# Sums and splits moved from GpSimd to VectorE, squares to ScalarE, renamed blocks and new planner costs in a fused retention, expert and feed-forward kernel

## The chip, the cores and the metric

One core of a Trainium2 chip. The metric is device time in microseconds (us) of that core, the median of several executions. "The profiled execution" is one execution recorded by the hardware profiler. The trace uses the engine names PE (TensorE matmuls), PEld (its weight loads), DVE (VectorE), ACT (ScalarE), POOL (GpSimd) and SP (the queue that issues most DMAs).

## What is computed

Three blocks follow each other, on 4,608 tokens (8 sequences of 576, 8 heads of width 64, model width 512):

```python
ret = (scale * q @ k.T) * Dmat                  # decayed, causal retention
x   = (ret @ v), heads joined                   # [4608, 512]
logits = x @ w_gate + modality_bias[modality_id]
e = argmax(logits); g = softmax(logits)[e]
x   = g * (relu(x @ w1[e]) @ w2[e])             # one expert of 8 per token, width 1024
h   = relu(x @ w_in)                            # dense, width 2048
out = (h * h) @ w_out
```

All arithmetic of the reference is float32. The last two blocks are worked out with each float32 operand split into a high part in a rounded format and the rest (hi and lo), three matmuls per product.

## The kernel before

The program runs in three stages on one core.

**Retention stage** (`phase0`, the first 195 us). Token tiles of 128, with routing tables built alongside. The change does not touch it.

**Expert stage** (`phase12`, 195 to 698 us). Tokens are gathered by expert into slots of 512 tokens ("E", 0 to 7) and a last slot of 256 (number 8). A slot has 8 units, and the loop at the end of `phase12` runs over all 80 units `i`. In each unit it emits `first` of the next unit (12 matmuls, then ACT writes `hh` and DVE writes `hl`), `second` of this one (12 matmuls), at four units of a slot the transposes of the next slot's gathered tokens (`trans`, tile `xg`), one expert weight's split (`wsplit`: ACT writes the high part of `wx` or `wy`, DVE the rest) and, through `part(cs, ...)`, a piece of the **conversion**. The gather (`gather`) is four indirect DMAs from POOL's queue, emitted in the first unit of a slot for the next.

The conversion (`convs`) turns the dense weights `w_in` and `w_out`, which arrive as 64-bit floats, into float32 and then into hi and lo blocks. It runs for 16 pieces; of each, `conv1` loads `craw`, `conv2` has six DVE steps on `cwk` (L693 to L707), one ACT square (L698) and four block sums of 256 columns (L715), and `conv3` splits the seven blocks in two parts of 768 and 1024 columns (`split`: ACT writes `cwh` at L149, the given engine `cwl` at L150) and stores them to `wc`. Each `yield` in it is one step (six per piece). Before, `part(cs, 2 if i >= 15 else 0)` runs two steps per unit from unit 15 on, so that the 99 steps take 50 units, and the sums and the splits' lower parts are on POOL.

`combos` makes the seven operand blocks of the dense stage's first token tile from the finished slot E (tile `eyr`), stores them to `xc`, and `preload` reads them back in unit 66.

**Dense stage** (`phase3`, from 698 us). Three passes over 9 token tiles of 512; in a pass, each tile meets three groups (`q`) of the hidden width, in the last pass two. Per group, a seven-product block scheme (Winograd's form of Strassen's) takes two matrix products: `one` has seven products `x`, `two` has seven, each of 6 matmuls of 256 columns. Between them DVE, ACT and POOL turn the seven results of `one` into blocks `z` (relu and square in `sq`, L1099; sums by `tt`, L1096) and split them into `h` (`hsplit`: ACT at L1213, DVE at L1214). `two`'s results are added up in `oe` or `yr`. In pass 0 `xprep` makes the next tile's operand blocks `x` (sums on POOL, splits on ACT and DVE); in the last pass POOL issues the indirect output DMAs (L1250).

The order of the dense stage is written by a list scheduler, `Plan`: every operation has a cost per engine (`a_`, `d_`, `p_`, `m_`) and its dependencies; `emit` picks the operation that can start first by these costs and thereby fixes the order in each engine's queue. An operation with two engines in its list goes to the one where it would end first. Each engine then runs its queue strictly in that order.

```python
            d_ = lambda c: [(DVE_, 0.153 + 0.00104 * c)]
            p_ = lambda c: [(POOL_, 0.10 + 0.00186 * c)]
                    tt(z[:, 3, :], z[:, 1, :], z[:, 0, :], ALU.subtract, 256, kz_(0, 1), kz_(3), p_(256) + d_(256))
```

Of the kernel before, what the change touches and what calls it, by code (L numbers as in the profile page):

```python
# [9 lines left out]
F32 = mybir.dt.float32  # L10
# [5 lines left out]
ALU = mybir.AluOpType  # L16
# [72 lines left out]
def kernel(ctx, tc, qT, kT, kN, vN, modT, w_gate, mbias, w1, w2, w_in, w_out,  # L89
# [574 lines left out]
    def phase12():  # L664
        with ExitStack() as c1:
# [5 lines left out]
            def conv1(i):  # L671
                fp, m = i // 2, i % 2
                raw = CR[i] = cv.tile([P, 2, 2 * CV], I32, tag="w", name="craw")
                for s_ in range(2):
# [4 lines left out]
                    else:  # L679
# [3 lines left out]
                        for j in range(2):  # L683
                            sp.dma_start(dst[:, j], src[s_, :, j])

            def conv2(i):
# [8 lines left out]
                yield 1  # L695
# [3 lines left out]
                yield 1  # L699
                dve.tensor_scalar(out=i1, in0=i2, scalar1=-(1 << 23), scalar2=None, op0=ALU.bitwise_and)  # L700
                yield 1
                dve.scalar_tensor_tensor(out=t1, in0=lw.bitcast(U32), scalar=2.0 ** -52, in1=t1,
                                         op0=ALU.mult, op1=ALU.mult)
                yield 1
                dve.tensor_tensor(out=t2, in0=t2, in1=t1, op=ALU.add)
                yield 1
# [6 lines left out]
                         (7, 3, ALU.subtract, 5)))[i % 2]  # L713
                for o, a, op, b in sums:
                    pool.tensor_tensor(out=bl[o], in0=bl[a], in1=bl[b], op=op)  # L715
                yield 1

            def conv3(i, part):
# [3 lines left out]
                split(ch, cl, src, pool)  # L722
# [21 lines left out]
            def combos():  # L744
                yr = cv.tile([P, KD, TS], F32, tag="w", name="eyr")
                tx = cv.tile([P, 3, 2, 256], F32, tag="w", name="etx")
                sp.dma_start(yr, yd[:, 0:TS].rearrange("(c p) t -> p c t", p=P))
                yield 1
                b11, b12 = yr[:, 0:2, 0:256], yr[:, 0:2, 256:512]
                b21, b22 = yr[:, 2:4, 0:256], yr[:, 2:4, 256:512]  # L750
                for o, a, b in ((tx[:, 0], b12, b11), (tx[:, 1], b22, tx[:, 0]), (b12, b22, b12),
                                (tx[:, 2], b21, tx[:, 1])):
                    pool.tensor_tensor(out=o, in0=a, in1=b, op=ALU.subtract)
                    yield 1
                src = (b11, b21, b22, tx[:, 0], tx[:, 1], b12, tx[:, 2])
                for m in range(7):
                    if m % 2 == 0:
                        xo = cv.tile([P, 2, 2, 2, 256], F32R, tag="w", name="exo")
                    split(xo[:, m % 2, 0], xo[:, m % 2, 1], src[m], dve)
                    sp.dma_start(xc[0, m], xo[:, m % 2].bitcast(F32).rearrange("p a k t -> p (a k t)"))  # L760
                    yield 1

            def preload():
                wload2(0, 0, cv)
                for a in range(4):
                    t_ = cv.tile([P, 2, 2, 2, 256], F32R, tag="w", name=f"x{a}")
                    for m in range(2 * a, min(2 * a + 2, 7)):
# [83 lines left out]
            def convs():  # L851
# [3 lines left out]
                for i in range(NCV + 1):  # L855
# [10 lines left out]
                    for n, _ in enumerate(conv2(i)):  # L866
                        if i and n in (2, 4):
                            conv3(i - 1, n // 4)
# [465 lines left out]
```

## Time and profile before

| | us |
|---|---|
| median of 3 runs (range) | 1500.33 (1497.33 to 1505.33) |
| the profiled execution: its own time | 1501.8 |
| the profiled execution: span of its instructions | 1500.0 |
| PE busy | 1390.7 (93% of the span) |
| DVE busy | 1089.3 (73%) |
| ACT busy | 579.9 (39%) |
| POOL busy | 503.8 (34%) |

A busy time is a union over the span; a busy PE is not a PE at its peak, since matmuls are pipelined. So the text also counts matmuls per stretch. PEclk is the share of TensorE's full clock that was granted: 1.00 is 2.4 GHz, and the lower level of 1.2 GHz counts as 0.50.

### The profile page before, as it was taken

Reading aid. Unit: us, or ns where it says so; the run is one execution under the profiler, and the core shown is the slowest. Engines: PE = TensorE matmul, PEld = TensorE weight load, DVE = VectorE, ACT = ScalarE, POOL = GpSimd, SP = SyncE. Lnnn points to the kernel's source line nnn. Section 1 sums busy time; section 2 is a strip of 40 time slices with the busy share of each in tenths; the row PEclk is TensorE's granted clock in tenths of the full one; section 3 lists DMA queues with packets and bytes.
Section 4 is the critical chain, followed back from the end, with each engine's and each line's share of the span. In section 5 each row is a group of like instructions: output and inputs, shape, how many; then the busy total and the mean of one; then the engine's idle time right before and its main releaser. Section 6 shows DMA issues by size and latency. Waiting matters only on the chain. (4 is left out here: it accounts for less than half of the span.)

```text
span 1500.0 us, 26403 instructions
## 1 busy us (share of the span) xinstructions
PE 1390.7 (93%) x10384; PEld 1263.5 (84%) x10384; DVE 1089.3 (73%) x1744; ACT 579.9 (39%) x1152; POOL 503.8 (34%) x440
## 2 busy tenths in 40 slices
PE   7999999979998989998799999999999999998994
PEld 6889878857776777778799999998999999998994
DVE  3776764649988988843688888867767777686784
ACT  1444443424444444432355444543223332233331
POOL 2222102216555555600434434322112222144354
PEclk9999999989999999999999999999999999999998
DMA  9977247868798889698644455576445564677672
GB/s 343 346 264 277 84 150 195 286 143 214 281 266 247 273 270 274 197 353 199 250 155 155 180 192 215 216 291 227 155 160 194 197 220 157 232 259 275 231 252 87
DMA packets 144743, 336.08 MB, mean 224 GB/s; under 512 B 20321, under 2 KB 54625, under 8 KB 144609
## 3 DMA queue, kind: packets, MB, share of 16 engines
q1 hardware_dynamic: 136528, 313.73, 62.2%
q0 software_dynamic: 5920, 19.40, 3.4%
q8 instruction: 83, 1.36, 0.4%
q10 hardware_dynamic: 2160, 1.17, 0.3%
q14 instruction: 52, 0.42, 0.1%
HBM read 226.24 MB, written 108.02 MB: 223 GB/s over the span
## 5 line engine op out<-in xcount | busy, mean ns | idle before, releaser
L1096 POOL TENSOR_TENSOR z<-z 128x256 f32<-128x256 f32 x176 | 178.9, 1018 | 421.7 <-DVE z L1096 381.7
L1114 PE MATMUL bank<-w,h 128*128 128x256 f32 x1008 | 288.8, 286 | 24.7 <-DVE h L1214 24.7
L1112 PE MATMUL bank<-w,h 128*128 128x256 f32 x1008 | 287.5, 285 | 14.8 <-ACT h L1213 11.9
L1112 PE MATMUL bank<-x,w 128*128 128x256 f32 x1008 | 285.9, 284 | 0.9 <-ACT z L1093 0.9
L1113 PE MATMUL bank<-x,w 128*128 128x256 f32 x1008 | 286.1, 284 | 0.1
L1113 PE MATMUL bank<-w,h 128*128 128x256 f32 x1008 | 284.2, 282 | 1.5 <-DMA w<-wc 1.3
L1114 PE MATMUL bank<-x,w 128*128 128x256 f32 x1008 | 284.9, 283 | 0.0
L1214 DVE TENSOR_TENSOR h<-z,h 128x512 fp32r<-128x512 f32 (+2 forms) x243 | 213.9, 909 | 10.3 <-ACT h L1213 10.1
L1114 PEld LDWEIGHTS bank<-w,h 128*128 128x128 f32 x1008 | 191.1, 190 | 35.1 <-DVE h L1214 35.1
L1213 ACT ACTIVATE h<-z 128x512 fp32r<-128x512 f32 (+2 forms) x243 | 155.5, 646 | 153.3 <-POOL z L1096 102.3
L1112 PEld LDWEIGHTS bank<-w,h 128*128 128x128 f32 x1008 | 191.5, 190 | 19.2 <-ACT h L1213 12.9
L1093 ACT ACTIVATE z<-bank 128x256 f32<-128x256 f32 x288 | 107.6, 380 | 256.9 <-PE bank L1114 256.3
L1113 PEld LDWEIGHTS bank<-x,w 128*128 128x128 f32 x1008 | 192.7, 191 | 1.2 <-DVE x L1096 0.3
L1112 PEld LDWEIGHTS bank<-x,w 128*128 128x128 f32 x1008 | 192.4, 191 | 1.6 <-ACT z L1093 1.4
L1113 PEld LDWEIGHTS bank<-w,h 128*128 128x128 f32 x1008 | 191.2, 190 | 2.1 <-DMA w<-wc 2.1
L1114 PEld LDWEIGHTS bank<-x,w 128*128 128x128 f32 x1008 | 192.8, 191 | 0.0
L775 PE MATMUL bank<-hh,wy 128*128 128x512 f32 (+1 forms) x320 | 131.2, 410 | 15.3 <-ACT hh L791 14.1
L1099 DVE SCALAR_TENSOR_TENSOR z<-z 128x256 f32<-128x256 f32 (+1 forms) x216 | 126.1, 585 | 23.4 <-ACT z L1093 17.2
L776 PE MATMUL bank<-hl,wy 128*128 128x512 f32 (+1 forms) x320 | 128.7, 402 | 6.7 <-DVE hl L792 6.7
L777 PE MATMUL bank<-hh,wy 128*128 128x512 f32 (+1 forms) x320 | 127.4, 398 | 0.0
L775 PE MATMUL bank<-xh,wx 128*128 128x512 f32 (+1 forms) x320 | 124.0, 388 | 2.2 <-PEq L888 1.7
L776 PE MATMUL bank<-xl,wx 128*128 128x512 f32 (+1 forms) x320 | 123.8, 387 | 0.7 <-DVE xl L742 0.7
(167 smaller groups left out, 2414.5 us busy)
## 6 DMA issues: line engine op xcount, KB each, us to landing
x<-xc SPq DMA_DIRECT2D x119, 512.0 KB
wr<-w SPq DMA_DIRECT2D x80, 512.0 KB
w<-wc SPq DMA_DIRECT2D x32, 896.0 KB
xc<-x SPq DMA_DIRECT2D x56, 512.0 KB
wc<-cwh SPq DMA_DIRECT2D x16, 896.0 KB
wc<-cwl SPq DMA_DIRECT2D x16, 896.0 KB
pd<-oe SPq DMA_DIRECT2D x24, 512.0 KB
xd<-xs SPq DMA_DIRECT2D x9, 1024.0 KB
```

Source lines behind the costliest of these rows:

```text
L775: pe.matmul(ps, lh, rh, start=first, stop=False)
L776: pe.matmul(ps, lh, rl, start=False, stop=False)
L777: pe.matmul(ps, ll, rh, start=False, stop=last)
L1093: plan.add(a_(c), lambda e: e.activation(o, i, AF.Copy), r, w)
L1096: plan.add(engs or d_(c), lambda e: e.tensor_tensor(out=o, in0=a, in1=b, op=op), r, w)
L1099: plan.add(d_(c), lambda e: e.scalar_tensor_tensor(out=z, in0=z, scalar=0.0, in1=z, op0=ALU.max, op1=ALU.mult), k, k)
L1112: e.matmul(ps[n], lh, rh, start=first and n == 0, stop=False, skip_group_check=True)
L1113: e.matmul(ps[n], lh, rl, start=False, stop=False, skip_group_check=True)
L1114: e.matmul(ps[n], ll, rh, start=False, stop=True, skip_group_check=True)
L1213: plan.add(a_(c), lambda e: e.activation(h[:, 0, a:b], z[:, a + 1:b + 1], AF.Copy), rs, ks[0])
L1214: plan.add(d_(c), lambda e: e.tensor_tensor(out=h[:, 1, a:b], in0=z[:, a + 1:b + 1], in1=h[:, 0, a:b].bitcast(F32), op=ALU.subtract), rs + ...
```

## The change

- In the conversion, the four block sums and the lower part of the splits go from POOL to DVE. The steps are no longer counted one by one: each `yield` gives a number of columns, and `part(cs, 2250)` hands out 2,250 columns per unit from unit 4 on; the 137,336 columns take 61 units. The two parts of `conv3` come one step earlier within the next piece.
- The copies of a slot's results out of PSUM (`ye`) are all on ACT; before, every other one was on DVE.
- `combos` runs at unit 68 and after, on DVE and ACT, and writes the operand blocks where the dense stage reads them; `preload` with its reading back from `xc` is gone, and the first dense weights are loaded in unit 73 instead of 66.
- In the dense stage the blocks `z` and `h` are renamed (`MH`; the two halves of `w_out` trade places in `conv1`, `dst[:, 1 - j]`), so that the `h` blocks that the first products of `two` read are made from other products of `one`. All sums of `z` are on DVE alone. The product `x == 4` is squared by ACT (relu on the way out of PSUM, then Square in place); the other three squares may go to DVE, or to ACT as two operations.
- The planner's costs change: ACT, DVE and above all POOL (for 256 columns from 0.58 to 0.87 us), and the handover between engines from 0.2 to 0.25 us.

```diff
             def conv2(i):
...
                 for o, a, op, b in sums:
-                    pool.tensor_tensor(out=bl[o], in0=bl[a], in1=bl[b], op=op)
-                yield 1
+                    dve.tensor_tensor(out=bl[o], in0=bl[a], in1=bl[b], op=op)
+                    yield 300
 
             def conv3(i, part):
...
-                split(ch, cl, src, pool)
+                split(ch, cl, src, dve)
...
+                sub(tx, b12, b11)
+                put(0, b11)
+                yield 1
...
                     for c in cols:
-                        if c % 2:
-                            act.activation(ye[:, c, :wd], Y[s, c][:, :wd], AF.Copy)
-                        else:
-                            dve.tensor_copy(ye[:, c, :wd], Y[s, c][:, :wd])
+                        act.activation(ye[:, c, :wd], Y[s, c][:, :wd], AF.Copy)
...
+            spare = [0]
+
             def part(gen, n):
-                while n and next(gen, 0):
-                    n -= 1
+                spare[0] = min(spare[0] + n, 2 * n)
+                while spare[0] > 0:
+                    c_ = next(gen, 0)
+                    if not c_:
+                        return
+                    spare[0] -= c_
                     yield
...
-                    fill(wsg(i + 6, 2 if i < 10 else 1, i + 9), part(cs, 2 if i >= 15 else 0))
-                    if 9 <= i <= 14:
-                        run(ex, 2)
-                    if i == 66:
-                        preload()
+                    fill(wsg(i + 6, 2 if i < 10 else 1, i + 9), part(cs, 2250))
+                    if i >= 68:
+                        run(ex, 3)
+                    if i == 73:
+                        assert next(cs, 0) == 0 and next(ex, 0) == 0
+                        wload2(0, 0, cv)
...
-    MH = {1: 0, 2: 1, 7: 2, 4: 3, 5: 4, 6: 5, 3: 6}
+    MH = {1: 0, 4: 1, 2: 2, 5: 3, 6: 4, 7: 5, 3: 6}
...
-        HAND = 0.2
+        HAND = 0.25
...
-            a_ = lambda c: [(ACT_, 0.17 + 0.00086 * c)]
-            d_ = lambda c: [(DVE_, 0.153 + 0.00104 * c)]
-            p_ = lambda c: [(POOL_, 0.10 + 0.00186 * c)]
+            a_ = lambda c: [(ACT_, 0.21 + 0.00083 * c)]
+            d_ = lambda c: [(DVE_, 0.15 + 0.00106 * c)]
+            p_ = lambda c: [(POOL_, 0.20 + 0.0026 * c)]
...
+                    if e is act:
+                        e.activation(z, z, AF.Relu)
+                        e.activation(z, z, AF.Square)
+                    else:
+                        e.scalar_tensor_tensor(out=z, in0=z, scalar=0.0, in1=z, op0=ALU.max, op1=ALU.mult)
...
-                    copy(z[:, 1, :], X_, 256, [kx], kz_(1))
-                    sq(z[:, 0:2, :], 512, kz_(0, 1))
-                    tt(z[:, 3, :], z[:, 1, :], z[:, 0, :], ALU.subtract, 256, kz_(0, 1), kz_(3), p_(256) + d_(256))
...
+                    copy(z[:, 3, :], X_, 256, [kx], kz_(3), AF.Relu)
+                    copy(z[:, 3, :], z[:, 3, :], 256, kz_(3), kz_(3), AF.Square)
+                    hsplit(u, z, h, 2 if last else 0, 3, kz_)
...
+                    tt(z[:, 4, :], z[:, 0, :], z[:, 2, :], ALU.add, 256, kz_(0, 2), kz_(4))
+                    if last:
+                        hsplit(u, z, h, 3, 4, kz_)
+                    tt(z[:, 5, :], z[:, 4, :], z[:, 1, :], ALU.subtract, 256, kz_(4, 1), kz_(5))
+                    hsplit(u, z, h, 4 if last else 3, 5, kz_)
```

The order that the change makes is shown at three places. The first is POOL's queue in the expert stage, around the gather for one slot (`xg` is the tile of gathered tokens, `ix` its indices, `cwk` and `cwl` the conversion's). Before:

```order
L150 TENSOR_TENSOR cwl<-cwk,cwh 128x768
L150 TENSOR_TENSOR cwl<-cwk,cwh 128x1024
L715 TENSOR_TENSOR cwk<-cwk 128x2x128 x4
L429 TENSOR_LOAD slots
L429 ISA x2
L431 ISA
L431 COPY ix<-tab 128x4
L434 DMA xg<-xd,ix 128x512 x4
L150 TENSOR_TENSOR cwl<-cwk,cwh 128x768
L150 TENSOR_TENSOR cwl<-cwk,cwh 128x1024
```

Now:

```order
L434 DMA xg<-xd,ix 128x512 x4
L429 TENSOR_LOAD slots
L429 ISA x2
L431 ISA
L431 COPY ix<-tab 128x4
L434 DMA xg<-xd,ix 128x512 x4
```

Between two gathers nothing else stands in POOL's queue any more.

The second is DVE's queue in the dense stage, second pass, around the end of `one` and the start of `two` (`z` and `h` are the blocks of three groups in turn, `bank` PSUM). Before:

```order
L1214 TENSOR_TENSOR h_9179<-z_9182,h_9179 128x512
L1214 TENSOR_TENSOR h_9178<-z_9181,h_9178 128x512
L1099 SCALAR_TENSOR_TENSOR z_9183<-z_9183 128x512
L1096 TENSOR_TENSOR z_9183<-z_9183,bank_88 128x256
L1099 SCALAR_TENSOR_TENSOR z_9183<-z_9183 128x256
L1096 TENSOR_TENSOR z_9183<-z_9183 128x256
L1214 TENSOR_TENSOR h_9180<-z_9183,h_9180 128x512
L1214 TENSOR_TENSOR h_9179<-z_9182,h_9179 128x512
L1214 TENSOR_TENSOR h_9180<-z_9183,h_9180 128x512
L1096 TENSOR_TENSOR oe<-oe,bank_85 128x2x256
```

Now:

```order
L1111 TENSOR_TENSOR z_9172<-z_9172,bank_88 128x256
L1236 TENSOR_TENSOR h_9169<-z_9172,h_9169 128x256
L1119 SCALAR_TENSOR_TENSOR z_9172<-z_9172 128x256
L1236 TENSOR_TENSOR h_9168<-z_9171,h_9168 128x512
L1111 TENSOR_TENSOR z_9172<-z_9172 128x256 x2
L1236 TENSOR_TENSOR h_9167<-z_9170,h_9167 128x512
L1236 TENSOR_TENSOR h_9169<-z_9172,h_9169 128x256 x2
L1111 TENSOR_TENSOR oe<-oe,bank_85 128x2x256
L1111 TENSOR_TENSOR z_9171<-z_9171 128x256 x2
L1111 TENSOR_TENSOR z_9172<-z_9172 128x256 x2
```

The sums of the last group (the rows `z<-z` without a bank) now stand in DVE's queue between its splits, and the last group's splits are cut into pieces of 256 columns. Of the 216 squares that have a choice, the order has 207 on DVE and 9 on ACT; 72 more stand on ACT by name.

The third is the DMA queue of SP at the end of the expert stage (`w` are the dense weights' tiles, `x` the operand blocks, `wr` the experts' weights). Before:

```order
L997 DMA w_5679<-wc 128x1792
L997 DMA w_5681<-wc 128x1792
L769 DMA x_5683<-xc 128x1024 x2
L769 DMA x_5686<-xc 128x1024 x2
L769 DMA x_5689<-xc 128x1024 x2
L769 DMA x_5692<-xc 128x1024
```

Now:

```order
L750 DMA eyr<-yd 128x4x512
L762 DMA xc<-x_5726 128x1024 x2
L400 ISA
L400 DMA wr_5772<-w 128x2x512
L762 DMA xc<-x_5727 128x1024 x2
L762 DMA xc<-x_5728 128x1024
L400 ISA
L400 DMA wr_5820<-w 128x4x256
```

The seven loads of `x` are gone; in their place the same bytes are stored, some units later, behind the load of `eyr` on which the new blocks depend.

## Rows read from the trace of the kernel before

**Rows 1.** The page, part 1: busy time, share of the span, instructions of each engine

```profile
PE 1390.7 (93%) x10384; PEld 1263.5 (84%) x10384; DVE 1089.3 (73%) x1744; ACT 579.9 (39%) x1152; POOL 503.8 (34%) x440
```

**Rows 2.** Busy time by stretch: PE, PEld, DVE, ACT, POOL (instructions), PEclk, DMA share, GB/s

```profile
300.00:640.00 340.00, 309.01 (x1306) 242.47 (x1304) 279.71 (x232) 139.20 (x185) 173.78 (x124) 0.95 0.80 241
640.00:698.00 58.00, 50.28 (x294) 44.65 (x295) 19.59 (x29) 14.94 (x27) 0.00 (x0) 0.91 0.91 298
698.00:740.00 42.00, 34.03 (x263) 33.04 (x262) 28.38 (x45) 17.21 (x36) 13.11 (x11) 0.92 0.68 198
740.00:1290.00 550.00, 532.50 (x4359) 521.83 (x4357) 425.07 (x709) 225.13 (x464) 164.75 (x149) 1.00 0.53 197
1290.00:1486.00 196.00, 179.24 (x1433) 173.62 (x1433) 150.25 (x244) 59.77 (x126) 81.39 (x82) 0.99 0.67 236
740.00:750.00 10.00, 10.00 (x86) 10.00 (x85) 5.85 (x12) 4.68 (x10) 4.34 (x4) 1.00 0.87 350
```

**Rows 3.** PE's waits, expert stage (195 to 698): us in total, times, longest

```profile
PE bank L775 <- ACT hh L791: 14.1, 2, 10.6
PE bank L739 <- DMA xg<-xd,ix: 13.8, 13, 1.6
PE bank L776 <- DVE hl L792: 6.7, 6, 2.4
```

**Rows 4.** PE's waits, dense stage (698 to 1486)

```profile
PE bank L1114 <- DVE h L1214: 24.7, 49, 1.7
PE bank L1112 <- ACT h L1213: 11.9, 5, 7.0
```

**Rows 5.** Timeline of DVE at the conversion's start: start, us, instruction, [idle before]

```profile
314.88 0.69 DVE L693 TENSOR_SCALAR cwk<-craw 128x1024 uint32<-128x1024 uint32 x1 [15.29 <-DMA craw<-w_in]
```

**Rows 6.** Timeline of POOL and of DVE around 417 us

```profile
411.77 1.80 POOL L434 DMA_INDIRECT xg<-xd,ix  x1 [0.27 <-POOL ix L431]
...
417.43 4.20 POOL L150 TENSOR_TENSOR cwl<-cwk,cwh 128x768 fp32r<-128x768 f32 x2
...
417.22 5.49 DVE L702 SCALAR_TENSOR_TENSOR cwk<-craw,cwk 128x1024 f32<-128x1024 uint32 x1
```

**Rows 7.** DVE's groups, shapes apart: busy us, mean ns of one, idle before

```profile
L1214 DVE TENSOR_TENSOR h<-z,h 128x512 fp32r<-128x512 f32 x171 | 152.6, 911 | 4.2 <-ACT h L1213 4.0
L1099 DVE SCALAR_TENSOR_TENSOR z<-z 128x256 f32<-128x256 f32 x144 | 70.4, 489 | 4.4
L150 DVE TENSOR_TENSOR wx<-wr,wx 128x1024 fp32r<-128x1024 f32 x40 | 68.4, 1711 | 9.2 <-ACT wx L149 8.6
L1096 DVE TENSOR_TENSOR oe<-oe,bank 128x512 f32<-128x512 f32 x97 | 65.5, 682 | 72.3 <-PE bank L1114 68.4 <-ACT oe L1093 2.6 <-issue 0.7
L1099 DVE SCALAR_TENSOR_TENSOR z<-z 128x512 f32<-128x512 f32 x72 | 55.9, 776 | 19.0 <-ACT z L1093 17.2
L1096 DVE TENSOR_TENSOR z<-z 128x256 f32<-128x256 f32 x112 | 47.6, 425 | 3.8
```

**Rows 8.** Tiles craw (ns min/median/max), xg (us to landing), cwk (DVE, ACT, POOL busy)

```profile
L702 DVE SCALAR_TENSOR_TENSOR cwk<-craw,cwk x16: 1224/1226/5494, 321.3 to 619.1; 128x1024 f32<-128x1024 uint32 x16
...
DMA to landing us min/median/max: 4.7/7.6/14.5
...
300.00:640.00 340.00, 146.65 (x96) 30.50 (x32) 145.01 (x96) 0.95 0.80 241
```

**Rows 9.** POOL's groups, shapes apart

```profile
L1096 POOL TENSOR_TENSOR z<-z 128x256 f32<-128x256 f32 x176 | 178.9, 1018 | 421.7 <-DVE z L1096 381.7 <-DVE z L1099 30.8 <-ACT z L1093 2.7
L150 POOL TENSOR_TENSOR cwl<-cwk,cwh 128x1024 fp32r<-128x1024 f32 x16 | 44.5, 2780 | 15.1 <-ACT cwh L149 15.0
```

**Rows 10.** Timeline of ACT at the dense stage's start

```profile
721.45 0.63 ACT L1093 ACTIVATE x<-yr 128x512 fp32r<-128x512 f32 x1 [7.89 <-DMA yr<-yd]
```

**Rows 11.** Timeline of POOL and ACT in the last pass

```profile
1385.91 0.99 POOL L1250 DMA_INDIRECT out<-yr,ix  x1 [4.85 <-DMA out<-yr,ix]
...
1387.70 0.42 ACT L1213 ACTIVATE h<-z 128x256 fp32r<-128x256 f32 x1 [5.45 <-POOL z L1096]
```

More of the change, by code (lines that the diff above doesn't have):

```diff
@@ L744, in combos @@
             def combos():
+                for _ in cs:
+                    pass
                 yr = cv.tile([P, KD, TS], F32, tag="w", name="eyr")
[L746 removed]
+                tx = cv.tile([P, 2, 256], F32, tag="w", name="etx")
                 sp.dma_start(yr, yd[:, 0:TS].rearrange("(c p) t -> p c t", p=P))
                 yield 1
+                xs = [cv.tile([P, 2, 2, 2, 256], F32R, tag="w", name=f"x{a}") for a in range(4)]
                 b11, b12 = yr[:, 0:2, 0:256], yr[:, 0:2, 256:512]
@@ L763, in preload, with sub @@
[L763 to L767, printed above, removed]
-                        held["x", m] = t_[:, m % 2]
-                        sp.dma_start(t_[:, m % 2].bitcast(F32).rearrange("p a k t -> p (a k t)"), xc[0, m])
+                def sub(o, a, b):
+                    dve.tensor_tensor(out=o, in0=a, in1=b, op=ALU.subtract)
@@ new lines, in put @@
+                def put(m, src):
+                    t_ = held["x", m] = xs[m // 2][:, m % 2]
+                    split(t_[:, 0], t_[:, 1], src, dve)
+                    sp.dma_start(xc[0, m], t_.bitcast(F32).rearrange("p a k t -> p (a k t)"))
+                sub(tx, b12, b11)
+                put(0, b11)
+                yield 1
+                put(1, b21)
+                yield 1
+                sub(b12, b22, b12)
+                put(2, b22)
+                yield 1
+                sub(b11, b22, tx)
@@ L771, in phase12 @@
+                put(3, tx)
+                yield 1
+                put(5, b12)
+                yield 1
+                sub(b21, b21, b11)
+                put(4, b11)
+                yield 1
+                put(6, b21)
+                yield 1
             HS = {}
@@ L1179, in one @@
                          [("w", 0, q, 0), ("w", 0, q, 1), ("x", mx, 0), ("x", mx, 1)], [kp])
+                last = q == len(PASSES[p]) - 1
                 if x == 1:
+                    copy(z[:, 1, :], X_, 256, [kx], kz_(1))
+                elif x == 2:
+                    tt(z[:, 1, :], z[:, 1, :], Z_, ALU.add, 256, [kz] + kz_(1), kz_(1))
+                    sq(z[:, 1, :], 256, kz_(1))
+                elif x == 6:
+                    copy(z[:, 0, :], X_, 256, [kx], kz_(0))
+                elif x == 7:
```

77 lines of the change are left out of this document (27 added, 50 removed).

## Prediction

> **What bounds the kernel now.** I read the page's busy times first [rows 1]: PE is at 93%, so what can be won is PE's idle time and the time at the lower clock, and nothing that merely shortens another engine's work counts. The table by stretch comes next [rows 2]. The reader should see where PE is not full. From 300 to 640 us (most of the expert stage) PE is idle for 340.0 - 309.0 = 31 us, and a PEclk of 0.95 takes another 0.05 x 340 = 17 us. From 640 to 698 it is 7.7 us idle and 0.09 x 58 = 5 us of clock; from 698 to 740, where the dense stage starts, 8.0 and 3.4 us. In the dense stage "busy" hides short waits, so I count matmuls: an undisturbed 10 us hold 86, hence 740 to 1290 with 4,359 needs 507 us and takes 550 (43 us lost), and 1290 to 1486 with 1,433 needs 167 and takes 196 (29 us lost). Retention, 0 to 195, is untouched.
>
> Then PE's waits. In the expert stage three kinds add up to 34.6 us [rows 3]: for ACT's `hh` 14.1 (one of 10.6), for the gathered tokens `xg` 13.8, for DVE's `hl` 6.7. The timelines show what is behind each. The long `hh` wait is the conversion's first piece: DVE stood 15.3 us for the load of `craw` [rows 5], with the next units' work queued behind. The `xg` waits come from POOL's queue: around 412 us the four gathers stand between the conversion's sums and splits, and start only when those are through [rows 6]. The `hl` waits come from DVE: an operation with a median of 1.23 us [rows 8] took 5.49, from 417.22 to 422.71, while two POOL splits ran from 417.43 to 421.63 [rows 6]. In the dense stage 36.6 us are waits for `h` [rows 4]; 7.0 of it is one wait at the start, where ACT stood 7.89 us for the load of `yr` with splits behind it [rows 10], and one in the last pass comes from POOL: an output DMA waited 4.85 us, and the block sums queued behind it came so late that ACT's split idled 5.45 us [rows 11].
>
> **The change, part by part.**
>
> *POOL against DVE.* The row first: the same DVE operation takes 1.22 us at least and 5.49 at most, the longest one exactly while POOL works in SBUF [rows 6, 8]; splits of 512 columns average 911 ns, where an addition of 512 columns out of PSUM takes 682 [rows 7]. The Trainium skill, page "SBUF — State Buffer", section "SBUF: two separate sides", says that VectorE operations with two SBUF inputs and GpSimd operations share one port pair under an exclusive lock, the loser waiting for the whole instruction. By that rule all of the excess goes with POOL's work; by the mean rows alone none would. The 5.49 us in the trace agree with the rule. I take the short durations from the rows, and keep the means as the other bound.
>
> *Expert stage, DVE's load.* Added: 64 sums of 256 columns at 0.425 [rows 7] = 27 us; 16 lower parts of 1,024 columns at 1.23 [rows 8] = 20; 16 of 768 columns at about 0.95 (estimate, between 0.682 for 512 and 1.23) = 15; together 62. Removed: 18 result copies at 0.68 (a full-size addition out of PSUM takes 0.682 [rows 7]) = 12. The conversion's own 96 steps take 146.7 us [rows 8]; at 1.23 each at most 118. The `wx` splits would fall from 1.711 to 1.23, 19 us over 40 [rows 7]. So the conversion costs DVE (118 + 62)/61 = 2.95 us per unit, against 146.7/50 = 2.93, and all else gets 0.5 us per unit lighter. From 300 to 640 pass some 52 units (1,306 matmuls, 24 for a unit and now and then a few transposes): DVE works 279.7/52 = 5.4 us in each, and would work 4.9 of the (340 - 31 - 17)/52 = 5.6 us that a unit takes when PE neither waits nor slows. That is 87%, tight but enough. With the mean durations kept (splits at 1.71, additions of the conversion near 75 us) it would be (147 + 75)/61 = 3.6, hence 5.4 - 2.9 + 3.6 - 0.2 = 5.9 us: too much. ACT has 139 of 340 us [rows 2]; 20 more copies of 0.6 lie beside other work.
>
> *Expert stage, waits.* POOL's 145 us of conversion work [rows 8] leave its queue, so a gather starts at once; four land within 5 + 7.6 us, 14.5 at the worst [rows 8], where three units (17 us) stand before the transposes. I count the 13.8 us as gone. The first conversion load now stands in unit 4, still one unit ahead of its use, but seven stores of 512 KB that went before it in SP's queue are now at the end of the stage; I expect a DVE stand of a few us that PE's unit in hand covers, and count the 10.6 as gone. Of the 6.7 for `hl` I count 4. Of the 31 us idle that makes 25, of the 17 us of lower clock (which follow these gaps) 12. New on the path: at unit 68 the splits for the first operand blocks wait in DVE's and ACT's queues for the 1 MB load of `eyr` issued just ahead. Before, POOL alone waited there. The nearest rows bound it: 0, or the 10.6 of `craw` [rows 3] and its clock, about 17; I take 2, since at this point the conversion's traffic is over. The first dense weights, 3.6 MB from unit 73 on, need 12 us at the 298 GB/s of that stretch [rows 2], and seven half-size units lie ahead of the dense stage: hidden. With 3 us of `xg` and its clock from 640 to 698, the expert stage gives 25 + 12 + 3 - 2 = 38 us. The 7.7 us around the branch for further slots stay for the most part.
>
> *Dense stage.* DVE: 176 sums come from POOL at 0.425 = +75; 72 squares of 512 columns at 0.776 go = -56; 207 - 144 squares of 256 at 0.425 come = +27; splits of 512 fall to 0.682, 171 x 0.229 = -39; squares of 256 fall from 0.489 to 0.425, -9 [rows 7]. Sum -2 us: the load on DVE stays at about 604 of 788 us [rows 2]. What goes is the chain: sums at 1.018 on POOL [rows 9] become 0.425, without two handovers. The first product of `two` reads a block that is ready early; the last block's chain now has about five groups of PE work (6 matmuls at 10/86 = 0.116 us, 0.7 us) as cover instead of two or three. And no block sum stands behind an output DMA any more. Of the 43 us lost from 740 to 1290 I take 16 (by length of stretch two thirds of the 24.7 us [rows 4] lie there), of the 29 us in the last pass 12. The start (8.0 and 3.4 us) stays: `yr` still waits for the last result's store and for four weight loads, and ACT's queue still holds a split behind it. Dense stage: 28 us, with bounds of -5 (every wait returns in DVE's queue) and 45.
>
> *Sum.* 38 + 28 = 66 us of the profiled 1501.8 give 1436; that execution lies 1.5 us above the median, inside the runs' range, so 1436 stands for the median too. Differences under 0.5% (7.5 us) can't be told from no change here.
>
> **The rivals.**
>
> *One stage only* (1464): the dense stage gives nothing, since waits for POOL's sums become waits in DVE's queue. For: POOL still takes its `xprep` sums in pass 0, and DVE has more small pieces in one queue. Against: 1.018 against 0.425 [rows 7, 9]. Chance 0.16.
>
> *Gathers held up by DVE* (1455): the `xg` waits stay, 13.8 us and about 5 of clock. For: the first gather instruction took 1.80 us while DVE worked [rows 6]. The Trainium skill, same page and section, has the rule of which this is the result: while VectorE runs a two-port operation, GpSimd is locked out and cannot write descriptors. Against: even 14.5 us to landing fit into three units. Chance 0.09.
>
> *DVE's queue becomes the bound* (1511, the other side): in the dense stage DVE has 604 us of work in 72 groups, 8.4 us each, and PE needs 14 x 0.7 = 9.8; the idle time in which DVE waits for PSUM in `oe` alone is 72.3 us [rows 7], 1.0 per group. From the point at which its waits for ACT and PE pass 1.4 us per group, DVE and not PE sets the pace. At 2.8 us a group takes 11.2, 72 make 806, with the 11 us of the start 817 in place of 788; in the expert stage 5.9 us per unit (above) wins 340 - 52 x 5.9 = 33 us, less the 17 of a stand at unit 68. Together 1501.8 + 29 - 16 = 1515. Against: both stages would have to keep the long durations with POOL's work gone. Chance 0.07.
>
> *More than forecast* (1415): the start's 11 us and half of the rest in the last pass go as well. Chance 0.12.
>
> *The change doesn't do what it says* in part: 207 of 216 squares stay on DVE, which is in the sum. That POOL's load or the durations fed to the planner move nothing that PE waits for (within 0.5%): 0.05.
>
> **How the numbers follow.** The forecast, 1420 to 1453 around 1436, has 0.51, and the time is its own. The range 1412 to 1474 takes in the two milder rivals and the greater gain, with the bounds of the `eyr` wait and of the dense stage partly, and leaves out the rest. Faster by over 0.5%: 0.51 + 0.16 + 0.09 + 0.12 = 0.88, less 0.01 for their edges, 0.87; same 0.06; slower 0.07.
>
> **What would show it.** Right: PEclk near 1.00 from 300 to 640 and under 4 us of `xg` waits; splits of 512 columns at about 0.69; the expert stage at about 465 us instead of 503; 81 or more matmuls per 10 us in the two first passes of the dense stage. Wrong: DVE over 92% busy from 250 to 640; a PE wait of over 5 us at unit 68; waits for `h` still near 25 us in the dense stage; an `L693` stand at unit 5 as long as the old one.

## The result and the profile after

The changed kernel takes 1432.72 us (median of 4 runs, 1429.32 to 1434.05), the kernel before 1502.19 (4 runs): a ratio of 0.9537, 95% interval 0.9503 to 0.957. The forecast was 1436 in a range of 1412 to 1474. The profiled execution took 1429.32 us, its span is 1427.6.

I cut each profiled execution at the first transposed tokens, the first matmul on dense operand blocks and the last one:

| us | retention | expert stage | dense stage | its three passes | tail |
|---|---|---|---|---|---|
| before | 195.2 | 503.2 | 787.3 | 294.9, 286.3, 206.0 | 14.4 |
| after | 190.4 | 467.3 | 753.9 | 289.0, 269.1, 195.8 | 15.9 |
| difference | -4.8 | -35.9 | -33.4 | -5.9, -17.2, -10.2 | +1.5 |

Both stages gave about what was forecast (38 and 28 us). The three passes are counted by matmuls, 2,268 in each of the first two. The 4.8 us of retention belong to no part of the change: its code is the same, and in the twelve profiles of the experiments it took 193.3 to 195.3.

Part 1 of the page of the changed kernel, against [rows 1] (busy us, share, instructions): POOL has lost 322 us of work, DVE only 63.

```profile
PE 1359.1 (95%) x10384; PEld 1250.9 (88%) x10384; DVE 1026.1 (72%) x2018; ACT 632.1 (44%) x1289; POOL 182.0 (13%) x164
```

Its table by stretch, against [rows 2] (us, then PE, PEld, DVE, ACT, POOL busy with instructions, PEclk, DMA share, GB/s):

```profile
300.00:640.00 340.00, 332.05 (x1532) 269.45 (x1531) 251.29 (x314) 159.72 (x224) 28.41 (x28) 0.99 0.88 257
640.00:660.00 20.00, 15.35 (x92) 14.79 (x93) 3.11 (x7) 2.84 (x9) 0.00 (x0) 0.66 0.80 320
660.00:700.00 40.00, 32.98 (x251) 31.81 (x251) 26.38 (x50) 18.25 (x39) 5.77 (x4) 0.91 0.64 181
740.00:1220.00 480.00, 474.94 (x3979) 472.65 (x3978) 364.17 (x768) 228.57 (x490) 40.33 (x22) 1.00 0.55 202
1220.00:1412.00 192.00, 180.93 (x1478) 178.35 (x1477) 145.70 (x312) 72.23 (x161) 32.98 (x32) 0.98 0.71 253
```

From 300 to 640 us PE is idle for 8 us (before 31) at a clock of 0.99 (before 0.95), and 1,532 matmuls pass instead of 1,306. From 740 to 1220 there are 82.9 matmuls in 10 us where before there were 79.3. The row from 640 to 660 stands out: 4.7 us idle and a clock of 0.66, and of the 8 us idle in the row above it, 5.6 lie in its last ten. This place at the end of the expert stage isn't new, it got worse. The kernel before has it from 680 to 700:

```profile
680.00:700.00 20.00, 13.84 (x93) 13.08 (x92) 3.59 (x7) 3.52 (x8) 0.00 (x0) 0.83 0.79 278
```

PE's waits in the expert stage (195 to 670), against [rows 3], then in the dense stage (655 to 1425), against [rows 4] (us in total, times, longest):

```profile
PE bank L787 <- ACT hh L803: 5.7, 1, 5.7
PE bank L787 <- PEq L904: 3.9, 1, 3.9
PE bank L740 <- DVE hl L804: 2.1, 2, 1.7
PE bank L740 <- DMA xg<-xd,ix: 1.2, 1, 1.2
...
PE bank L1133 <- ACT h L1235: 5.8, 1, 5.8
PE bank L1133 <- DVE yr L1111: 5.0, 2, 3.3
PE bank L1134 <- DVE x L1111: 4.1, 5, 0.9
PE bank L1133 <- DVE oe L1111: 3.1, 4, 0.9
PE bank L1135 <- DVE h L1236: 1.1, 3, 0.5
```

The `xg` waits fell from 13.8 to 1.2 us, the waits for `h` from 36.6 to 6.9, and 5.8 of those are the single one at the start of the dense stage.

DVE's groups with shapes apart, against [rows 7, 8] (busy us, mean ns of one, idle before and its releaser):

```profile
L1236 DVE TENSOR_TENSOR h<-z,h 128x512 fp32r<-128x512 f32 x144 | 100.4, 706 | 10.1 <-ACT h L1235 10.1
L1119 DVE SCALAR_TENSOR_TENSOR z<-z 128x256 f32<-128x256 f32 x207 | 92.8, 449 | 6.2
L150 DVE TENSOR_TENSOR wx<-wr,wx 128x1024 fp32r<-128x1024 f32 x40 | 48.8, 1221 | 24.9 <-ACT wx L149 24.1 <-issue 0.3
L716 DVE TENSOR_TENSOR cwk<-cwk 128x256 f32<-128x256 f32 x64 | 24.7, 421 | 0.8
L702 DVE SCALAR_TENSOR_TENSOR cwk<-craw,cwk 128x1024 f32<-128x1024 uint32 x16 | 19.6, 1224 | 0.4
L150 DVE TENSOR_TENSOR cwl<-cwk,cwh 128x1024 fp32r<-128x1024 f32 x16 | 19.5, 1219 | 0.3 <-ACT cwh L149 0.3
```

Splits of 512 columns went from 911 to 706 ns, `wx` from 1,711 to 1,221, and the `L702` step never takes longer than 1.23 us.

### The profile page after: what moved, and what is told of

It reads as the page before. It is cut to its first block, busy times and chain, and to the rows that moved or that the text cites. A ratio compares the mean times of both kernels' runs of the same rounds, so it can differ in the third digit from the quotient of the medians.

```text
span 1427.6 us, 26428 instructions
## 1 busy us (share of the span) xinstructions
PE 1359.1 (95%) x10384; PEld 1250.9 (88%) x10384; DVE 1026.1 (72%) x2018; ACT 632.1 (44%) x1289; POOL 182.0 (13%) x164
## 5 line engine op out<-in xcount | busy, mean ns | idle before, releaser
L1133 PE MATMUL bank<-w,h 128*128 128x256 f32 x1008 | 285.5, 283 | 16.1 <-ACT h L1235 5.8
L1236 DVE TENSOR_TENSOR h<-z,h 128x512 fp32r<-128x512 f32 (+2 forms) x270 | 173.3, 661 | 12.1 <-ACT h L1235 11.7
L1111 DVE TENSOR_TENSOR z<-z,bank 128x256 f32<-128x256 f32 x216 | 90.2, 418 | 63.1 <-PE bank L1135 42.3
L787 PE MATMUL bank<-hh,wy 128*128 128x512 f32 (+1 forms) x320 | 126.9, 397 | 5.7 <-ACT hh L803 5.7
L787 PE MATMUL bank<-xh,wx 128*128 128x512 f32 (+1 forms) x320 | 124.6, 389 | 3.9 <-PEq L904 3.9
L788 PE MATMUL bank<-hl,wy 128*128 128x512 f32 (+1 forms) x320 | 124.4, 389 | 1.0 <-DVE hl L804 1.0
L789 PE MATMUL bank<-xh,wx 128*128 128x512 f32 (+1 forms) x320 | 124.0, 388 | 0.0
L789 PE MATMUL bank<-hh,wy 128*128 128x512 f32 (+1 forms) x320 | 123.7, 387 | 0.0
```

Of the source, the lines that this page charges most:

```text
L787: pe.matmul(ps, lh, rh, start=first, stop=False)
L788: pe.matmul(ps, lh, rl, start=False, stop=False)
L789: pe.matmul(ps, ll, rh, start=False, stop=last)
L1111: plan.add(engs or d_(c), lambda e: e.tensor_tensor(out=o, in0=a, in1=b, op=op), r, w)
L1133: e.matmul(ps[n], lh, rh, start=first and n == 0, stop=False, skip_group_check=True)
L1236: plan.add(d_(c), lambda e: e.tensor_tensor(out=h[:, 1, a:b], in0=z[:, a + 1:b + 1], in1=h[:, 0, a:b].bitcast(F32), op=ALU.subtract), rs + ...
```

## The experiments

They ran on chips on which the kernel before took 1510 to 1517 us. Its dense stage was as long there as in the first profile (787.6 in e3, which leaves it alone), its expert stage longer (518.0 and 519.5 in e4 and e6, which leave that alone). So totals are told as ratios, and stages are held against these and against e5. One profile gives a stage to a few us only: the changed kernel's own dense stage was 753.9 in the first and 759.2 in e5. "A" is the theory that moving the work between engines wins the time, "B" that the early and even spreading does, "C" that the renamed blocks and their order do.

### The changed kernel once more (e5)

> The changed kernel once more, unchanged, as the reference for the three others on this chip. All theories: 0.950 to 0.957 of the kernel before, expert stage 465 to 470 us, dense stage 752 to 756.

1443.79 us, 0.9527 [0.9494, 0.9559]; stages 472.1 and 759.2, passes 292.3, 269.1, 197.7. The ratio is that of the first comparison, but both stages are longer than expected, by 2 to 3 us. The ranges of e7 and e8, put on record with e5's, have to be read against this run.

### The conversion back on GpSimd (e1)

```diff
-                    dve.tensor_tensor(out=bl[o], in0=bl[a], in1=bl[b], op=op)
+                    pool.tensor_tensor(out=bl[o], in0=bl[a], in1=bl[b], op=op)
...
-                split(ch, cl, src, dve)
+                split(ch, cl, src, pool)
```

> The changed kernel, with the conversion's block sums and the lower part of its splits back on GpSimd, still spread from unit 4 on. Theory A (the engine move gives the expert stage its gain, by the freed queue and the shared access to SBUF): gathers wait behind sums again and VectorE's steps are stretched; waits for xg 8 us or more, expert stage 485 to 500 us (467 in the changed kernel, 503 before), time 1450 to 1465. Theory B (the gain comes from starting earlier and spreading more evenly): expert stage 465 to 473, time 1430 to 1440. Dense stage unchanged at 754 by both.

1478.5 us, 0.9765 [0.9737, 0.9793]; expert stage 512.5. Nearly the whole gain of that stage is lost, more than A had expected. PE's waits in e1's expert stage (195 to 712):

```profile
PE bank L740 <- DMA xg<-xd,ix: 29.1, 22, 5.0
PE bank L787 <- ACT hh L803: 6.8, 1, 6.8
```

The waits that are new are those for gathered tokens: 29 us where e5 has none. The other 11 of the 40 us against e5 are for the most part clock (a PEclk of 0.95 over the stage, against 0.97). Whether GpSimd's queue holds up the gathers or its work slows VectorE this run doesn't tell; e9 does.

### The late start (e2), and the conversion on VectorE alone (e3)

e2 is the changed kernel with the conversion starting at unit 15, as before:

```diff
-                    fill(wsg(i + 6, 2 if i < 10 else 1, i + 9), part(cs, 2250))
+                    fill(wsg(i + 6, 2 if i < 10 else 1, i + 9), part(cs, 2750 if i >= 15 else 0))
```

> The changed kernel, with the conversion started at unit 15 instead of 4 and 2,750 columns per unit, so that it ends at the same unit. Theory A: VectorE has some 5.5 of 5.6 us per unit, little is lost; expert stage 465 to 475, time 1430 to 1441. Theory B: the stage goes back most of the way, 485 or more, time 1450 or more.

e3 is the kernel before, with the conversion's sums and splits on VectorE and nothing else:

```diff
-                    pool.tensor_tensor(out=bl[o], in0=bl[a], in1=bl[b], op=op)
+                    dve.tensor_tensor(out=bl[o], in0=bl[a], in1=bl[b], op=op)
...
-                split(ch, cl, src, pool)
+                split(ch, cl, src, dve)
```

> The kernel before, with the conversion's sums and splits on VectorE and nothing else changed (two steps per unit from unit 15). Theory A: the waits for xg and hl go, the first load's wait of 10.6 us and its time at the lower clock stay; expert stage 474 to 486, time 1473 to 1485. Theory B: VectorE is over its budget (3.6 us of conversion per unit) and the stage stays at 500 or more, time 1500 or more. Dense stage 787 by both.

e2: 1467.37 us, 0.9692 [0.9652, 0.9732], expert stage 495.3. e3: 1493.56, 0.9865 [0.9836, 0.9893], expert stage 495.2. So the late start, with the denser spread that goes with it, costs 23 us even with all else changed, and the move alone wins 23 of the 46 by which the stage is shorter in e5 than in e4 and e6. e2 is as B had it; e3 lies between the two theories and meets neither. In both the `xg` waits are gone and others stand in their place: in e3 18.9 us for `hh` and 11.7 for `hl`. PE's waits in e2 (195 to 665), and DVE's timeline at the first conversion load (start, us, instruction, idle before):

```profile
PE bank L787 <- ACT hh L803: 13.1, 2, 11.5
PE bank L740 <- DVE hl L804: 7.6, 5, 2.3
PE bank L788 <- DVE hl L804: 3.7, 5, 2.1
...
315.51 0.70 DVE L693 TENSOR_SCALAR cwk<-craw 128x1024 uint32<-128x1024 uint32 x1 [16.14 <-DMA craw<-w_in]
```

This stand is the 15.29 us of before [rows 5]. SP's timeline of e2 and of the changed kernel, at the two loads of `w_in` that the first piece needs and the four of `w_out` for the second:

```profile
296.99 1.37 SPq L677 DMA_DIRECT2D craw<-w_in  x2
299.83 13.12 SPq L684 DMA_DIRECT2D craw<-w_out  x4
```

```profile
224.63 0.98 SPq L677 DMA_DIRECT2D craw<-w_in  x2
230.19 5.28 SPq L684 DMA_DIRECT2D craw<-w_out  x4
```

In e2 no `xc` store stands in SP's queue, and yet DVE can start on the first piece only 18.5 us after the issue of its loads (296.99 to 315.51); in unit 4 it starts 10.3 us after (224.63 to 234.92) and stands for 5.18. It is the place that helps; what makes the same loads slower at the other place, no run shows.

### The gathers two units earlier, the conversion on GpSimd (e9)

e1, with the call that gathers the slot after next put behind unit 6's `second` (and only E's first left where it was):

```diff
-                if nx is not None and f == (4 if s == "E" else 0):
+                if s == "E" and f == 4:
                     gather(nx)
...
+                if f == 6 and k + 2 < len(seq):
+                    gather(seq[k + 2])
```

> The changed kernel with the conversion's sums and splits on GpSimd, as in e1, and each slot's gather put two units earlier into GpSimd's queue (unit 6 of the slot before, ahead of the conversion's pieces of units 6 and 7). e1 had an expert stage of 512.5 us, 40 over the changed kernel's 472 on such a chip, with 29 us of waits for xg. Theory Q (the gathers stand in GpSimd's queue behind sums and splits, and that is what is lost): waits for xg under 8 us, expert stage 472 to 488, total 1444 to 1460. Theory P (sums and splits on GpSimd slow VectorE, whose conversion instructions took 1.3 to 2.8 times as long in e1): waits for xg fall but hh and hl or others take their place, expert stage 498 to 515, total 1470 to 1487.

1440.86 us, 0.954 [0.9506, 0.9574]; expert stage 471.7, the changed kernel's 472.1 again. No wait for `xg` is left. The first gather of a slot on POOL and its first transposes on PE, in the timelines of e1 and then of e9 (start, us, instruction, idle before); under each, the tile `xg`'s time to landing from 200 to 640 us:

```profile
467.24 1.80 POOL L434 DMA_INDIRECT xg<-xd,ix  x1 [0.27 <-POOL ix L431]
482.60 0.33 PE L740 MATMUL bank<-ident,xg 128*128 128x128 f32 x1 [1.85 <-DMA xg<-xd,ix]
DMA to landing us min/median/max: 5.6/13.2/17.2
```

```profile
479.21 0.98 POOL L434 DMA_INDIRECT xg<-xd,ix  x1 [0.27 <-POOL ix L431]
506.97 0.60 PE L740 MATMUL bank<-ident,xg 128*128 128x128 f32 x4
DMA to landing us min/median/max: 5.1/6.7/7.8
```

In e1 the gather starts 15 us before its tokens are wanted and lands too late; in e9 it starts 28 us before. Over the slots after 300 us the lead is 13 to 22 us in e1, 24 to 34 in e9 and 39 to 42 in e5. With nothing else in POOL's queue a gather waits only for PE's transposes, as these rows of the changed kernel show:

```profile
461.65 0.97 POOL L434 DMA_INDIRECT xg<-xd,ix  x1 [14.10 <-PE bank L740]
501.23 0.60 PE L740 MATMUL bank<-ident,xg 128*128 128x128 f32 x4
```

The lead is not the whole of it. The fourth gather of e1's slot starts at 472.29 and PE comes for it at 480.75, so that with e9's landing of 6.7 us it would have been in time. The place in the queue did two things: it set the lead, and it put the transfers into a moment in which they took twice as long. POOL does the same work in both, and DVE is slowed by it in both (`L700`: a mean of 1,922 ns in e1, 1,721 in e9). The tile `cwk` in e9 and in the changed kernel (ns min/median/max, first and last start):

```profile
L700 DVE TENSOR_SCALAR cwk<-cwk x16: 681/2331/2898, 249.7 to 575.5; 128x1024 int32<-128x1024 int32 x16
L702 DVE SCALAR_TENSOR_TENSOR cwk<-craw,cwk x16: 1214/1226/3440, 250.4 to 577.9; 128x1024 f32<-128x1024 uint32 x16
L705 DVE TENSOR_TENSOR cwk<-cwk x16: 1210/1219/3443, 251.7 to 581.4; 128x1024 f32<-128x1024 f32 x16
```

```profile
L700 DVE TENSOR_SCALAR cwk<-cwk x16: 683/688/693, 243.3 to 565.9; 128x1024 int32<-128x1024 int32 x16
L702 DVE SCALAR_TENSOR_TENSOR cwk<-craw,cwk x16: 1219/1224/1227, 244.0 to 566.6; 128x1024 f32<-128x1024 uint32 x16
L705 DVE TENSOR_TENSOR cwk<-cwk x16: 1212/1219/1224, 245.3 to 571.2; 128x1024 f32<-128x1024 f32 x16
```

`L700` takes 2,331 ns instead of 688, and nothing comes of it: from 300 to 640 us DVE is 255.85 us busy in e9 and 253.86 in e5. (In e9 DVE is spared the sums and lower parts, some 60 us of work, and pays about as much in longer instructions; what it would do with both, no run shows.) Theory Q holds, with times slightly shorter than it had, and P falls.

### The dense stage taken apart (e4, e6, e7, e8)

e4 is the kernel before with the sums of `z` kept off GpSimd:

```diff
-                    e = p_(256) + d_(256)
+                    e = d_(256)
```

e6 is e4 with the planner's new costs, e7 the changed kernel with the old ones:

```diff
-        HAND = 0.2
+        HAND = 0.25
...
-            p_ = lambda c: [(POOL_, 0.10 + 0.00186 * c)]
+            p_ = lambda c: [(POOL_, 0.20 + 0.0026 * c)]
```

e8 is the changed kernel with all squares on VectorE:

```diff
-                plan.add(d_(c) + [(ACT_, 2 * a_(c)[0][1])], go, k, k)
+                plan.add(d_(c), go, k, k)
...
-                    copy(z[:, 3, :], X_, 256, [kx], kz_(3), AF.Relu)
-                    copy(z[:, 3, :], z[:, 3, :], 256, kz_(3), kz_(3), AF.Square)
+                    copy(z[:, 3, :], X_, 256, [kx], kz_(3))
+                    sq(z[:, 3, :], 256, kz_(3))
```

> The kernel before, with all block sums of the dense stage on VectorE alone, the planner's costs as they were. Theory A (GpSimd's slow sums and the splits that they stretch make the dense stage wait): dense stage 762 to 772 instead of 787, splits of 512 columns at 0.69 us, time 1475 to 1487. Theory C (the renamed blocks and the order that follows from them give the gain): the sums' time only moves into VectorE's queue, dense stage 782 to 792, time 1495 to 1507.

> The kernel before, with the dense sums on VectorE alone and the planner's new durations and hand-over time; blocks named and ordered as before, squares on VectorE. With these durations the planner gives no sum to GpSimd even if it may, so this is also the kernel before with nothing but new durations. The sums alone (old durations) had left the dense stage at 772. Theory D (what the planner believes of durations matters, since it decides the order): dense stage 756 to 765. Theory C (the renamed blocks and the order of their sums bring the rest): 768 to 776. Total by D 1480 to 1492 on a chip where the kernel before takes 1507, by C 1490 to 1500.

> The changed kernel with the planner's old durations and hand-over time of 0.2 us; everything else as changed (sums fixed to VectorE, so that none goes back to GpSimd). Theory D: dense stage 760 to 772, total 6 to 18 us over the changed kernel. Theory C: 752 to 757, total within 4 us of the changed kernel. Expert stage 465 to 470 by both.

> The changed kernel with all squares of the dense stage on VectorE (block 4 copied with Copy, then squared there). About 288 squares by 0.45 us are 40 to 60 us more on VectorE, which is some 55% busy in the last two passes and more in the first. Theory C (order and sums are what matters, VectorE has room): dense stage 753 to 758. Theory S (squares on ScalarE keep VectorE's queue short before the matmuls that wait for h): 762 to 775.

| | total, ratio | dense stage | passes |
|---|---|---|---|
| e4 | 1501.51, 0.9917 [0.9888, 0.9946] | 771.7 | 298.7, 271.6, 201.4 |
| e6 | 1507.35, 0.9936 [0.9912, 0.996] | 779.5 | 304.0, 272.9, 202.6 |
| e7 | 1443.95, 0.9539 [0.9517, 0.956] | 760.3 | 289.8, 269.8, 200.7 |
| e8 | 1446.78, 0.9555 [0.9533, 0.9577] | 762.3 | 294.3, 270.9, 197.0 |

Of the 28 us from 787.6 to e5's 759.2, the sums alone give 16, most of it in the second pass. By the letter e7 and e8 lie at the lower edge of D's and S's ranges, but those were laid round the first profile's 753.9. Against e5's 759.2 and 0.9527, neither the new costs (1 us) nor the squares on ScalarE (3 us) can be told from nothing, and in the old order the new costs win nothing either: e6 is longer than D and C both had it. D and S find no support, though 3 us for the squares aren't excluded. The other 12 us are a remainder. They don't come at the stage's start (231 matmuls in its first 40 us in e4, 224 in e5), but behind it, in the first pass (6.4 us in all) and in the last (3.7). What is left to explain them is the renamed blocks and their order, which no run tested by themselves. PE's waits in the dense stage of e4 (713 to 1490) show how far the sums go:

```profile
PE bank L1112 <- ACT oe L1093: 10.1, 7, 1.4
PE bank L1112 <- DVE oe L1096: 8.9, 7, 3.0
PE bank L1112 <- ACT h L1213: 7.4, 2, 6.9
PE bank L1114 <- DVE h L1214: 1.6, 3, 0.7
```

The 24.7 us for DVE's `h` [rows 4] are down to 1.6, but 19 us for the results `oe` have appeared, which in e5 are 6.8.

### The change of stages (e10, e11, e12)

In the changed kernel ScalarE's last weight split stood for its load. ACT's timeline of the changed kernel there and at the dense stage's start, against [rows 10]; ahead of it the same split in the kernel before:

```profile
682.93 1.06 ACT L149 ACTIVATE wy<-wr 128x1024 fp32r<-128x1024 f32 x1 [7.36 <-DMA wr<-w]
```

```profile
638.68 1.06 ACT L149 ACTIVATE wy<-wr 128x1024 fp32r<-128x1024 f32 x1 [9.55 <-DMA wr<-w]
681.32 0.63 ACT L1108 ACTIVATE x<-yr 128x512 fp32r<-128x512 f32 x1 [9.38 <-DMA yr<-yd]
```

e10 issues the seven `xc` stores after the last weight loads:

```diff
-                    sp.dma_start(xc[0, m], t_.bitcast(F32).rearrange("p a k t -> p (a k t)"))
+                    late.append((xc[0, m], t_.bitcast(F32).rearrange("p a k t -> p (a k t)")))
...
+            for o_, t_ in late:
+                sp.dma_start(o_, t_)
```

e11 is e10 with the planner's first transfer time set from 8 to 16 and the four sums of operand blocks (`p_(512)`, 32 over the pass) on VectorE (`d_(512)`):

```diff
-            plan.add([(DMA_, 8.0)], lambda e: None)
+            plan.add([(DMA_, 16.0)], lambda e: None)
...
-                tt(xt, b12, b11, sub, 512, [k12, k11], [("t",)], p_(512))
+                tt(xt, b12, b11, sub, 512, [k12, k11], [("t",)], d_(512))
```

e12 is the changed kernel with those sums on VectorE and the stores in the dense stage's plan, no longer in `put`:

```diff
             loadw(0, 1, 1)
+            for m in range(7):
+                dma(xc[0, m], XT[m].bitcast(F32).rearrange("p a k t -> p (a k t)"), 512,
+                    [("x", m, 0), ("x", m, 1)], [("xc", 0, m)])
```

> The changed kernel, with the seven stores of the first tile's operand blocks issued on SP's queue after the last weight loads instead of among them (units 68 on). In the changed kernel ScalarE waited 9.55 us for the last expert weight load, TensorE stood some 11 us at 634 to 648 and ran at 0.66 of its clock in the next stretch. Theory T (the stores hold up the last weight loads): that wait falls below 4 us, expert stage 4 to 10 us shorter (462 to 468 where the changed kernel takes 472), total 6 to 12 us less than the changed kernel. Rival (the loads are late for another reason, such as the buffer they need): expert stage 470 to 474, total within 3 us.

> As e10, and in the dense stage the 32 remaining sums of operand blocks (512 elements, 1.3 to 2.7 us on GpSimd, about 0.7 us on VectorE) on VectorE as well, and the planner told that the transfers before the first tile's loads take 16 us, not 8, so that ScalarE's queue doesn't stand for yr ahead of the first h. Theory: dense stage 8 to 14 us shorter than the changed kernel's on such a chip (759): the first pass 284 to 289 instead of 292, the rest the stall at its start. Rival (VectorE is the dense stage's next limit in the first pass, 80% busy there): first pass 292 to 298, dense stage 757 to 765.

> The changed kernel, with the seven stores of the first tile's operand blocks taken out of the expert stage and given to the dense stage's planner, behind the first pass's weight loads, and with the 32 sums of operand blocks on VectorE. e10 had shortened the expert stage by 6 us, and TensorE had then waited 9.1 us for weight blocks (w) that stood behind the stores at the start of the dense stage. Theory T (around the change of stages the transfers are the bound, and the stores, 3.6 MB, are the part that can wait): expert stage 464 to 468, wait for w under 3 us, first pass 282 to 290, total 8 to 16 us less than the changed kernel, ratio 0.942 to 0.949 of the kernel before. Rival (the loads of w alone set the start of the dense stage, and what was spared is lost there): first pass 292 to 299, total within 4 us of the changed kernel, ratio 0.951 to 0.957.

e10: 1443.83 us, 0.9572 [0.9539, 0.9606], stages 466.3 and 763.9. e11: 1443.04, 0.9565 [0.953, 0.9599], 469.1 and 761.6. By its expert stage e10 goes with T, by its total with the rival. ACT's longest stand for that load falls only to 7.1 us in e10, and the 6 us won in its expert stage are lost again at the start of the dense stage, whose last weight blocks are now issued behind the stores. PE's waits in e10 (650 to 1440):

```profile
PE bank L1136 <- DMA w<-wc: 9.1, 1, 9.1
```

e11's further edits change neither that nor the first pass by much (295.6 us against 292.3 in e5). The rival's reason for that, VectorE as the next limit, doesn't fit e12, which has the same sums on VectorE. e12: 1440.22 us, 0.9489 [0.9468, 0.951]; the first pass takes 283.9 us as expected and the dense stage 753.2, but the expert stage 474.2 instead of 464 to 468, where `wy` stood 8.5 us for its load again. So the stores are not what made that load late, or not alone, and the 6 us of e10's one profile are no proof that they were. The kernel before, without these stores at this place, has ACT stand 7.36 us for the same load. What all of them share is that six or eight loads of dense weights (896 KB each) are issued right behind it; no run moved those, and the cause stays open. e12 also changes two things at once, so that the shorter first pass can't be given to either. Its ratio is the lowest of all, but its interval overlaps e5's.

## Why the prediction was right, and where not

**What held.** The size of both stages in the first comparison (35.9 and 33.4 us; on the later chips, where the kernel before waits 22.1 us for `xg` in e4 and not 13.8, the expert stage gave 46 and the dense stage 28); PEclk near 1.00 and `xg` waits under 4 us from 300 to 640; the short durations on DVE (splits of 512 at about 0.69, measured 0.706); 81 or more matmuls in 10 us (82.9); the stall at the start of the dense stage (9.38 us on ACT against 7.89 [rows 10]); the 2 us for `eyr` at unit 68 (DVE stood 6.14 us, PE's gaps there are 0.38 and 1.08).

**The `hh` wait: gone, for another reason.** The step said that seven stores ahead in SP's queue made the first conversion load late. In e2 they are gone and DVE stands 16.1 us. The place in unit 4 is what helped. DVE's stand there isn't quite covered: PE waits 1.7 us for `hl` behind it in the first profile and 4.4 in e5.

**The first dense weights: mis-sized.** The step counted 3.6 MB, 12 us of loads, under seven half-size units. Eight loads of 896 KB stand there, 7.2 MB (six of them stood there before, too), and SP is busy with their issue for 24.93 us. ACT's last `wy` waited 9.55 us (before 7.36), PE 5.7 for `hh` (before 3.5), then 3.9 at the branch (before 1.7), and the granted clock was 0.66 for 20 us, a mean of its two levels (0.50 and 1.00), after PE had stood. These 20 us hold 4.7 us of idle time and 6.8 of clock; before, the 58 us from 640 to 698 held 7.7 and 5 [rows 2]. That the dense weights' loads hold up `wy` is argued, not shown. From 300 to 640 the gain was the forecast 37 us (23 of idle time and 14 of clock); what the sum had at +1 for the rest of the stage came out at about -1: that the total came so near is in part luck.

**DVE's load: enough, but not the reason.** The working put DVE's work at 87% of a unit, "tight but enough", if its operations get short. While the conversion runs DVE is 80% busy (251 of 315 us from 250 to 565), since two of the six steps take 0.69 us and not the 1.23 that all were given (100 us in place of 118). What it did not see is that the short durations weren't needed: in e9, with sums and splits still on POOL, DVE's steps are long, DVE is 79% busy (250 of the same 315), and the stage is the same. Nor do the `hl` waits, which the working laid on slow DVE operations, follow the durations: from 300 to 600 us they are 5.4 us before, 2.8 in e9 with long steps, 3.6 in e5 with short ones, and 10.5 in e2 and 10.6 in e3, whose steps are short too but stand denser.

The Trainium skill, page "SBUF — State Buffer", section "SBUF: two separate sides", has VectorE and GpSimd lock each other out of a shared port pair. The rows of e9 agree with it in the durations (`L700`, 688 to 2,331 ns). They also show that it decided nothing here: what PE waited for in this stage were the gathers, by their place in GpSimd's queue.

**The dense stage: term mis-sized by 5 us.** The sum took 16 us from the first two passes and 12 from the last; measured were 23 and 10. The long chain of sums was rightly named, but the runs give it 16 of the 28 us of e5; the other 12, by what is left, go to renaming and order, which the text had in one sentence about five groups of cover. DVE's work in this stage was to stay at 604 us and came to 569.

**The rivals.** *One stage only* fell with the table of stages. *Gathers held up by DVE* fell: they land 5.9 to 8.9 us after their issue in the changed kernel from 300 to 640. The 1.80 us that spoke for it [rows 6] were such a wait: the gather's instruction began at 411.77, during a VectorE step with two inputs (`L696`, 411.50 to 412.73), and ended 0.84 us after it. That this step is a two-port operation, as the working has it, no row shows; the changed kernel has gather instructions of up to 2.02 us as well, and PE doesn't wait for their tokens. *DVE's queue becomes the bound* fell, and e8, with 81 more squares in DVE's queue, does not come near; the heading of that rival says 1511 where its working ends at 1515. *More than forecast* (1415) didn't come: 1432.7 lies 3 us below 1436, and retention's 4.8 us, which are chance, are more than that.

## What to carry to other kernels

Where an engine's queue holds both work and the gathers that another engine waits for, look first at what stands ahead of each gather: issuing it two units earlier gave, with the same early and even spread, the same 46 us as moving the work to another engine. (No run has the early gathers without the early spread.) Slow instructions on an engine with a fifth of its time idle cost the expert stage nothing (e9), so a duration that will shrink is no gain until a wait is shown that ends on it. And a transfer taken out of a crowded stretch can be paid for right behind it (e10).

## What the runs showed of the hardware

**Sharing goes both ways.** POOL's subtraction `yr<-yr,xt` (512 columns) took a mean of 1,676 ns in the kernel before, 2,700 in the changed one and 3,176 in e4. It depends on what DVE does at that moment: in the changed kernel three of the eight took 1,295 to 1,613 ns beside one or two DVE instructions, and five 3,415 to 3,422 beside four, which then took 0.69 us each; before, the second of two DVE instructions beside it took 1.78 us. Groups of POOL, shapes apart, in the changed kernel and in e4:

```profile
L1111 POOL TENSOR_TENSOR yr<-yr,xt 128x512 f32<-128x512 f32 x8 | 21.6, 2700 | 120.0 <-ACT h L1235 83.2 <-DVE x L1111 19.5 <-ACT oe L1108 17.2
```

```profile
L1096 POOL TENSOR_TENSOR yr<-yr,xt 128x512 f32<-128x512 f32 x8 | 25.4, 3176 | 127.9 <-ACT h L1213 121.0 <-DVE x L1096 7.0
```

**Issue is not free.** Four loads of `w_out` occupy SP's queue for 5.28 us at 230 us of the changed kernel and 13.12 us at 300 of e2, with the same shapes. It is one of the four that holds the queue, for 2.96 and 10.58 us; the others take 0.6 to 1.0.

**A gather's landing depends on its moment.** In e1 it took 13.2 us in the median, in e9 6.7. The row of e1 starts 0.8 us behind a piece's two stores of 896 KB, but these alone don't hold a gather up: the one at 339.3 us of e9 starts 1.4 us behind such a pair and the last three of its four land 5.5 to 7.1 us after their issue. In six of e1's eight slots from 250 us on, the store of a slot's results (`yd`, 1 MB) is issued 5 to 9 us ahead of the gathers, in e9 behind them; that this is the cause isn't shown.
